# Moving the last quarter of w1's conversion behind the first products of a packed-attention mixer

## The chip, the cores and the metric

The kernel runs on one core of a Trainium2 chip. The metric is the device time of one launch in microseconds (us). Its engines are named as the profile names them: PE (TensorE, matrix products) with PEld (its weight loads), DVE (VectorE), ACT (ScalarE), POOL (GpSimd) and SP, the engine whose queue issues all of this kernel's transfers (SPq in the profile). Each engine works through its own instructions in order.

## The reference

An attention through 32 packed queries per head, then a token mix of low rank and a two-layer channel mix. Shapes: 8 batches, 8 heads, 576 tokens, head size 64, model width 512, hidden width 2048. U, V, w1 and w2 come as float64; the others as float32.

```python
def sm_attn(qq, kk, vv):                       # scale = 1/8
    s = scale * qq @ kk.T
    a = exp(s - max(s)); a = a / (sum(a) + 1e-9)
    return a @ vv
pp  = sm_attn(p, k, v)                         # 32 packed rows per head
x   = sm_attn(q, pp, pp)                       # (B, S, 512) after the heads are joined
h   = x.transpose(0, 2, 1) @ U @ V             # mixes tokens, rank 32
u   = x + h.transpose(0, 2, 1)
out = u + relu(u @ w1) @ w2
```

## The kernel before, in words

**First stage** (about the first 107 us). Sixteen *units* `u = (b, g)`, a batch and half of its heads each. For each unit the kernel loads a tile of k (`kx`, three buffers, `a_load`) and one of v (`vt`, three buffers, `a_load_v`), turns k on PE (`a_turn`, tiles `k_ps`), multiplies with the turned queries `pT` (`a_scores`, `s_ps`), takes maximum and exponential (`a_softmax`: DVE `mx`, ACT `e`), turns back, multiplies with v (`a_pack`: ACT `two`) and turns the packed rows (`a_heads`: ACT copies them into `ppTa`, one buffer, and SP stores `ppTa` to DRAM as `ppTd`). The raw packed queries `pn` are loaded for two batches at a time. Batch 0's own attention (`attention(0, res)`) runs among the units.

**Weights.** w1 and w2 are float64 in DRAM and are turned into float32 on the chip by `float32_of` (lines 71 to 82): one ACT instruction (absolute value, line 77 or 143) and four of DVE (lines 78 to 81) on a raw tile `bits` of 128x512 numbers, 512 KB. w1 has 16 such chunks, four for each quarter of the 2048 hidden columns. Before, all 16 are converted in the first stage, one after each unit's softmax and two at units 1, 5 and 9; each conversion (`some_w1`) is followed by the absolute value of the next chunk and the load of the third after it. Four chunks are loaded up front. The result stays in SBUF as `w1t`.

**Main stage.** For each batch `b` a loop over 16 steps `kt` of 128 hidden columns. `fold(b, c)` multiplies a quarter c of w1 with the batch's packed rows (line 372) and splits the result into a high and a low part, `wth` by ACT (line 378) and `wtl` by DVE (line 379); it runs at kt 2, 6, 10 and 14 for the quarter that is needed from the second step after on. So w1's last quarter is first read at kt = 10 of batch 0. `gemm1(kt)` makes the hidden columns in two PSUM banks `h_ps` (one buffer each, lines 86 to 88), ACT makes `hh` and `hj` of them (lines 611, 613) and DVE `hl` (line 614). `gemm1(kt + 1)` overwrites the same banks and so waits for `hl` of step kt. `gemm2(kt - 1)` (tiles `o`) follows `gemm1(kt)`.

**Batch 0 has more to do**: w2's 16 chunks are converted in it, one per step. At step kt `split_w2` writes the two parts of chunk kt + 1 (`w2h` by ACT, line 158; `w2l` by DVE, line 159), then chunk kt + 3 is loaded and chunk kt + 2 converted. The steps of `attention(1, res)` are handed out among these too (`steps`), and the tail of the last units (`rest`).

The order of the main stage is the order of the code (a manual schedule); the first stage's order is made by the framework's scheduler. Below, "step 3" means kt = 3 of batch 0, and gemm1(3) or hl(3) what belongs to it.

Of the kernel before, what the change touches and what calls it, by code (L numbers as in the profile page):

```python
# [8 lines left out]
F32 = mybir.dt.float32  # L9
F32R = mybir.dt.float32r  # L10
I32 = mybir.dt.int32
# [8 lines left out]
def packed_attention_mixer_kernel(  # L20
# [27 lines left out]
    nc = tc.nc  # L48
    B, H, S, D = q.shape
# [4 lines left out]
    P = 128  # L54
# [3 lines left out]
    NK = DF // P  # L58
    NU = 2 * B
    QW = 512  # L60
    NPC = DF // QW
# [7 lines left out]
    U, V, w1, w2 = (a.bitcast(I32) for a in (U, V, w1, w2))  # L69
# [35 lines left out]
    def ppT_tile():  # L105
        return pipe.tile([P, 2, P], F32, name="ppT", bufs=3)
# [6 lines left out]
    w1t = [pipe.tile([P, DF], F32, name=f"w1t{x}", tag=f"w1t{x}") for x in range(4)]  # L113
    w2t = {}

    def w2_tiles(pool, n):
        for i in range(n, n + 2):
            w2t[i] = tuple(pool.tile([P, 4, DM], F32R, name=f"w2{x}{i}", tag=f"w2{x}{i}", bufs=1) for x in "hl")
# [6 lines left out]
    def conv_tile(dtype):  # L125
        return pipe.tile([P, DM], dtype, name="os", bufs=4)
# [2 lines left out]
        return pipe.tile([P, 512, 2], I32, name="bits", bufs=2)  # L129

    chunks = [(x, c) for c in range(NPC) for x in range(4)]
    bits = {}

    def load_w1(n):
        x, c = chunks[n]
        b = bits["w1", n] = bits_tile() if n % 2 else sA.tile([P, 512, 2], I32, name="bits2")
        nc.sync.dma_start(out=b.rearrange("p x t -> p (x t)"), in_=w1[P * x:P * x + P, 2 * QW * c:2 * QW * c + 2 * QW])
# [15 lines left out]
    def convert_w2(kt):  # L153
        return kt, float32_of(conv_tile(I32), conv_tile(F32), bits.pop(("w2", kt)))
# [212 lines left out]
    def fold(b, c):  # L367
        f_ps = [bank() for _ in range(2)]
        for h in range(H):
            g, z = h // 4, h % 2  # L370
            xs, zs = slice(32 * (h % 4 ^ g), 32 * (h % 4 ^ g) + 32), slice(64 * z, 64 * z + 64)
            nc.tensor.matmul(f_ps[g][xs], lhsT=ppT[b][zs, g, xs], rhs=w1t[h // 2][zs, QW * c:QW * c + QW],  # L372
                             start=True, stop=True)
        for a in range(2):
            hi, lo = (pipe.tile([P, 2, QW // 2], F32R, name=f"wt{x}", tag=f"wt{x}", bufs=3) for x in "hl")
            cs = slice(QW // 2 * a, QW // 2 * a + QW // 2)
            for g in range(2):
                nc.scalar.copy(hi[:, g], f_ps[g][:, cs])  # L378
                nc.vector.tensor_tensor(lo[:, g], f_ps[g][:, cs], hi[:, g].bitcast(F32), op=ALU.subtract)  # L379
            wt[b, 2 * c + a] = hi, lo  # L380
# [6 lines left out]
    sT = tctx.enter_context(tc.tile_pool(name="sT", bufs=2, side="right", reuse_waits="tile"))  # L387
# [5 lines left out]
    pn, pT, pps, sums = {}, {}, {}, {}  # L393
# [4 lines left out]
    def a_load(u):  # L398
        b, g = UN[u]
        ua[u] = {}  # L400
        if u % 4 == 0:
            pn[b // 2] = sA.tile([P, 2, 2, D], F32, name="pn", bufs=1)
            nc.sync.dma_start(out=pn[b // 2], in_=p[b:b + 2].rearrange("b (g h) n d -> (h n) b g d", g=2))
        ua[u]["x"] = sA.tile([P, 2 * S], F32, name="kx", bufs=3)
        load_nat(ua[u]["x"], k, b, g)

# [10 lines left out]
    def a_p(b):  # L417
        t_ps = bank()
        pT[b] = sA.tile([P, 2, P], F32, name="pT")
        pd = sA.tile([P, 2, 2, D], F32, name="pd", bufs=1)  # L420
        nc.gpsimd.tensor_copy(pd, pn[b // 2][:, b % 2].unsqueeze(2).to_broadcast([P, 2, 2, D]))
        for i in range(2):
            nc.tensor.transpose(t_ps[:, P * i:P * i + P], pd[:, i].rearrange("p z d -> p (z d)"), ident)
        nc.scalar.activation(pT[b][:, 0], t_ps[:, :P], AF.Copy, scale=scale)
        dst, src = (a.rearrange("p (y z n) -> p z y n", y=2, z=2) for a in (pT[b][:, 1], t_ps[:, P:2 * P]))
        for z in range(2):
            nc.scalar.activation(dst[:, z], src[:, 1 - z], AF.Copy, scale=scale)
# [55 lines left out]
    def a_heads(u):  # L483
        b, g = UN[u]
        if g == 0:
            pps[b] = ppT_tile() if b == 0 else sT.tile([P, 2, P], F32, name="ppTa", bufs=1)
        z_ps = bank()
        nc.tensor.transpose(z_ps[:, :P], ua[u]["two"].rearrange("p z d -> p (z d)"), ident)
        nc.scalar.copy(pps[b][:, g], z_ps[:, :P])
        if g == 1:  # L490
            if b == 0:
                ppT[0] = pps[0]
            else:
                nc.sync.dma_start(out=ppTd[b], in_=pps[b].rearrange("p g n -> p (g n)"))
# [1 line left out]
    a_load(0)  # L496
    a_load(1)
    a_load_v(0)
    for n in range(4):
        load_w1(n)  # L500
    a_turn(0)
    first = attention(0, res)
    test_w1(0)

    def some_w1(n):
        convert_w1(n)
        if n + 1 < 16:
            test_w1(n + 1)
        if n + 4 < 16:
            load_w1(n + 4)  # L510

    n_w1 = 0
    for i in range(NU):
        if i > 0:
            a_turn_back(i - 1, bank_a("m"))
        a_scores(i)
        if i + 1 < NU:
            a_load_v(i + 1)
            a_turn(i + 1)
        if i + 2 < NU:  # L520
            a_load(i + 2)
        a_softmax(i)
        for _ in range(2 if i in (1, 5, 9) else 1):
            if n_w1 < 16:
                some_w1(n_w1)
                n_w1 += 1
        if i > 1:
            a_pack(i - 2, bank_a("m"))
        if i > 2:
            a_heads(i - 3)  # L530
        if i >= 4:
            for _ in range(3):
                if first:
                    first.pop(0)()
        if i == 2:
            uv = load_uv()
        if i == 3:
            prepare_uv(*uv)
        if i == 13:
            fold(0, 0)  # L540
        if i == 14:
            load_w2(0)
            load_w2(1)
            steps = attention(1, res)
            steps.pop(0)()
            split_w2(*convert_w2(0))
            load_w2(2)
# [111 lines left out]
    def joint(b, parts):  # L659

        oj = psO.tile([P, DM], F32, name="o", tag="o")
        for kt in range(NK):
            if kt % 4 == 0:
                hi, lo = parts.pop(0)
                if kt // 4 + 2 < NK // 4:
                    parts.append(joint_parts(b, kt // 4 + 2))
            cs = slice(P * (kt % 4), P * (kt % 4) + P)
            mm3(oj, (hi[:, cs], lo[:, cs]), w2_parts(kt), kt == 0, kt == NK - 1)
            if kt == 0:
                for i in range(2):  # L670
                    residual(oj, ajh[i], ajl[i], rdh[i], rdl[i])
        return oj

    def store_joint(b, oj):
        os_ = conv_tile(F32)
        nc.scalar.copy(os_, oj)
        for i in range(2):
            nc.sync.dma_start(out=out[b - 1 + i].rearrange("(i c) m -> c i m", c=NT)[8], in_=os_[I * i:I * i + I])

    w2x = convert_w2(1)  # L680

    for n in (20, 19, 18, 15, 15, 14, 13, 12, 12, 11, 5, 0, 0, 0, 0):
# [2 lines left out]
    for b in range(B):  # L685
        cur = Batch(b)
        oj = None
        ahead = attention(b + 2, res) if b + 2 < B else []
        for kt in range(NK):
            cur.gemm1(kt)  # L690
            if oj and kt == 1:
                store_joint(b - 1, oj)
            if steps and (b < 2 or kt % 4 != 2) and (b, kt) != (1, 0):
                steps.pop(0)()
            if (b, kt) == (0, 5):
                w2_tiles(ctx.enter_context(tc.tile_pool(name="sC", bufs=1, side="right", reuse_waits="tile")), 2)
            if kt > 0:
                cur.gemm2(kt - 1, (rest or steps).pop(0) if b == 0 and (rest or steps) else None)
            elif last:
                last.gemm2(NK - 1)  # L700
                last.store()
                if last.b % 2 == 1:
                    oj = joint(last.b, parts)
            if w2x:
                split_w2(*w2x)
                w2x = None
                if kt + 3 < NK:
                    load_w2(kt + 3)
                if kt + 2 < NK:
                    w2x = convert_w2(kt + 2)  # L710
            if kt % 4 == 2 and (b, kt) != (B - 1, NK - 2):
                n = b * NPC + kt // 4 + 1
                fold(n // NPC, n % NPC)
            elif steps and (b, kt) != (1, 0):
                steps.pop(0)()
            if kt == 1:
                cur.blocks()
            if kt == 3:
                cur.add_u()
            if ahead and kt == (13 if b else NK - 1):  # L720
                ahead.pop(0)()
            if kt == NK - 1 and b % 2 == 1:
                parts = [joint_parts(b, 0), joint_parts(b, 1)]
        assert not steps
        steps = ahead
        last = cur
# [35 lines left out]
```

## Time and profile before

| | before |
|---|---|
| time, median of 3 runs | 851.7 us (851.23 to 853.27) |
| time of the profiled execution | 849.79 us |
| its span, first to last instruction | 848.0 us |
| mean granted TensorE clock | 0.985 of full speed |
| busy in the span: PE / DVE / ACT / POOL | 815.2 / 381.2 / 327.8 / 86.1 us |
| start of gemm1(0), the main stage's first product | 107.39 us |

The page gives each engine's busy time and share, and the busy tenths in 40 slices of 21.2 us: PE stands at 9 in nearly all slices behind the fifth, DVE is high in the first nine and falls to 3 or 4 after them. The DMA engines are busy throughout the first four slices (tenths 9 9 9 9) and mostly idle later. The chain of work that ended last runs over PE for 85% of the span.

### The profile page before, as it was taken

To read this page: it belongs to the slowest core of one execution; us is meant where nothing else is said; L and a number is where in the kernel's file an instruction comes from. 1 tells how busy PE (TensorE), PEld (TensorE's weight loads), DVE (VectorE), ACT (ScalarE), POOL (GpSimd) and SP (SyncE) were. 2 spreads that over 40 slices of the span, in tenths; PEclk is the share of its full clock that TensorE was granted. 3 is DMA by queue.
4 is the path that set the end of the run, shared out by engine and by line. 5 is a ranking of instruction groups with operands and counts; after the bars stand their busy time and mean duration, and the time that the engine had idled before them with its cause. 6 is when DMAs were issued, how large, how long until landed. Compare 5 with 4: busy or idle time off the path is not lost.

```text
span 848.0 us, 14578 instructions
## 1 busy us (share of the span) xinstructions
PE 815.2 (96%) x5800; PEld 654.5 (77%) x5800; DVE 381.2 (45%) x902; ACT 327.8 (39%) x1017; POOL 86.1 (10%) x131
## 2 busy tenths in 40 slices
PE   5888789999999999999999999999999999999997
PEld 3555468788878878888888887888788888888786
DVE  5799576984343333434343234333434234342221
ACT  5677664445223333334333342333234322342231
POOL 1122210111111000110011001010101011000000
PEclk8799999999999999999999999999999999999999
DMA  9999632331001100011001100010001100010001
GB/s 306 353 346 313 229 104 71 104 131 50 1 1 63 51 13 1 1 63 50 1 2 63 50 14 1 17 61 36 1 3 61 63 1 1 2 50 1 1 1 63
DMA packets 36182, 58.13 MB, mean 69 GB/s; under 512 B 8977, under 2 KB 19217, under 8 KB 36113
## 3 DMA queue, kind: packets, MB, share of 16 engines
q1 hardware_dynamic: 36112, 57.19, 20.4%
q8 instruction: 46, 0.75, 0.4%
q14 instruction: 24, 0.19, 0.1%
HBM read 46.83 MB, written 10.35 MB: 67 GB/s over the span
## 4 chain that ended last, share of the span: by engine, by line
PE 85%; DVE 6%; DMA 4%; ACT 2%; issue 1%; SPq 1%; POOL 0%; ACTq 0%; POOLq 0%; DVEq 0%
PE o L86 16%; PE o L88 16%; PE o L87 16%; PE h_ps L86 8%; PE h_ps L88 7%; PE h_ps L87 7%; PE t_ps L372 4%; DMA vt<-in_v_dram 2%; DMA bits<-in_moe_w_ch_dram 2%; PE t_ps L224 2%; PE t_ps L244 1%; PE t_ps L320 1%; DVE os L80 1%; PE k_ps L224 1%; PE s_ps L244 1%
## 5 line engine op out<-in xcount | busy, mean ns | idle before, releaser
L86 PE MATMUL o<-w2h,hh 128*128 128x512 f32 x512 | 206.8, 404 | 0.0
L88 PE MATMUL o<-w2h,hl 128*128 128x512 f32 x512 | 202.5, 396 | 0.0
L87 PE MATMUL o<-w2l,hh 128*128 128x512 f32 x512 | 202.1, 395 | 0.0
L614 DVE SCALAR_TENSOR_TENSOR hl<-h_ps,hh 128x256 fp32r<-128x256 f32 x256 | 104.1, 423 | 203.3 <-ACT hj L613 191.2
L611 ACT ACTIVATE hh<-h_ps 128x256 fp32r<-128x256 f32 x256 | 99.0, 388 | 185.5 <-PE h_ps L88 184.9
L86 PE MATMUL h_ps<-ah,wth 128*128 128x320 f32 (+1 forms) x512 | 157.3, 307 | 1.7 <-DVE hl L614 1.7
L87 PE MATMUL h_ps<-al,wth 128*128 128x320 f32 (+1 forms) x512 | 151.7, 296 | 0.0
L88 PE MATMUL h_ps<-ah,wtl 128*128 128x320 f32 (+1 forms) x512 | 151.5, 296 | 0.0
L86 PEld LDWEIGHTS h_ps<-ah,wth 128*128 128x128 f32 x512 | 96.8, 189 | 33.3 <-issue 25.2
L88 PEld LDWEIGHTS o<-w2h,hl 128*128 128x128 f32 x512 | 96.5, 188 | 22.8
L86 PEld LDWEIGHTS o<-w2h,hh 128*128 128x128 f32 x512 | 96.8, 189 | 21.5 <-issue 4.6
L87 PEld LDWEIGHTS o<-w2l,hh 128*128 128x128 f32 x512 | 96.8, 189 | 16.7
L87 PEld LDWEIGHTS h_ps<-al,wth 128*128 128x128 f32 x512 | 96.9, 189 | 1.9
L88 PEld LDWEIGHTS h_ps<-ah,wtl 128*128 128x128 f32 x512 | 97.0, 190 | 0.0
L379 DVE TENSOR_TENSOR wtl<-t_ps,wth 128x256 fp32r<-128x256 f32 x128 | 48.5, 420 | 92.8 <-ACT wth L378 89.5
L378 ACT CAST wth<-t_ps 128x256 fp32r<-128x256 f32 x128 | 43.4, 374 | 111.1 <-PE t_ps L372 97.8
L335 POOL TENSOR_TENSOR al<-aT,ah 128x320 fp32r<-128x320 f32 (+1 forms) x32 | 25.9, 812 | 206.4 <-ACT ah L334 206.4
L283 POOL TENSOR_TENSOR e<-e,m 128x576 f32<-128x576 f32 x16 | 18.9, 1184 | 257.1 <-DVE m L282 257.1
L372 PE MATMUL t_ps<-w1t,ppT 64*32 64x512 f32 x512 | 36.8, 608 | 0.0
L231 ACT COPY xT<-t_ps 128x256 f32<-128x256 f32 x60 | 20.3, 394 | 39.6 <-PE t_ps L224 39.0
L334 ACT CAST ah<-aT 128x320 fp32r<-128x320 f32 (+1 forms) x32 | 13.8, 433 | 44.5 <-DVE aT L333 44.5
L294 POOL TENSOR_TENSOR e<-e,s 128x576 f32<-128x576 f32 x16 | 18.9, 1179 | 109.8 <-DVE s L293 102.7
(134 smaller groups left out, 964.2 us busy)
## 6 DMA issues: line engine op xcount, KB each, us to landing
bits<-in_moe_w_ch_dram SPq DMA_DIRECT2D x32, 512.0 KB, 6.3
kx<-in_k_dram SPq DMA_DIRECT2D x16, 576.0 KB, 7.2
x<-in_q_dram SPq DMA_DIRECT2D x16, 576.0 KB, 4.9
vt<-in_v_dram SPq DMA_DIRECT2D x32, 256.0 KB, 6.7
out_dram<-bits SPq DMA_DIRECT2D x32, 256.0 KB, 2.4
vt<-in_v_dram SPq DMA_DIRECT2D x16, 64.0 KB, 6.0
out_dram<-os SPq DMA_DIRECT2D x8, 128.0 KB, 2.3
ppTd<-ppTa SPq DMA_DIRECT2D x7, 128.0 KB, 4.0
```

Source lines behind the costliest of these rows:

```text
L86: nc.tensor.matmul(ps, lhsT=lh, rhs=rh, start=start, stop=False)
L87: nc.tensor.matmul(ps, lhsT=lh, rhs=rl, start=False, stop=False)
L88: nc.tensor.matmul(ps, lhsT=ll, rhs=rh, start=False, stop=stop)
L224: nc.tensor.transpose(t_ps[:, o:o + P], x[:, h, P * j:P * j + P], ident)
L231: nc.scalar.copy(dst, src[:, a])
L283: nc.gpsimd.tensor_tensor(e, e, m.unsqueeze(2).to_broadcast([P, S // 32, 32]), op=ALU.subtract)
L335: nc.gpsimd.tensor_tensor(al[:, g, ns], aT[:, ns], ah[:, g, ns].bitcast(F32), op=ALU.subtract)
L372: nc.tensor.matmul(f_ps[g][xs], lhsT=ppT[b][zs, g, xs], rhs=w1t[h // 2][zs, QW * c:QW * c + QW], start=True, stop=True)
L378: nc.scalar.copy(hi[:, g], f_ps[g][:, cs])
L379: nc.vector.tensor_tensor(lo[:, g], f_ps[g][:, cs], hi[:, g].bitcast(F32), op=ALU.subtract)
L611: nc.scalar.activation(hh[:, ms], src, AF.Relu)
L614: nc.vector.scalar_tensor_tensor(hl[:, ms], src, 0.0, hh[:, ms].bitcast(F32), op0=ALU.max, op1=ALU.subtract)
```

## The change

- The `pn` load brings one batch's packed queries instead of two, at every first unit of a batch.
- `ppTa` has two buffers instead of one.
- Two chunks of w1 are loaded up front instead of four. Units 0 and 1 convert nothing and load chunks 2 and 3; units 2 to 13 convert one chunk each: 12 chunks, three quarters of w1.
- The last quarter is converted in 8 halves of 128x256 numbers in batch 0, two in each of steps 3 to 6, called h0 to h7 below: one behind the first attention step of kt, one behind w2's conversion. A half's raw tile `wb` (256 KB) has one buffer. h0 is loaded at step 2; each conversion issues the load of the next half.
- In steps 2, 6, 10 and 14 the fold stands ahead of `split_w2` and w2's conversion, where it stood behind them.

```diff
+    NA = 4 * (NPC - 1)
+    halves = [(x, c, hf) for x, c in chunks[NA:] for hf in range(2)]
...
-        if u % 4 == 0:
-            pn[b // 2] = sA.tile([P, 2, 2, D], F32, name="pn", bufs=1)
...
+        if g == 0:
+            pn[b] = sA.tile([P, 2, D], F32, name="pn", bufs=1)
+            nc.sync.dma_start(out=pn[b], in_=p[b].rearrange("(g h) n d -> (h n) g d", g=2))
...
-            pps[b] = ppT_tile() if b == 0 else sT.tile([P, 2, P], F32, name="ppTa", bufs=1)
+            pps[b] = ppT_tile() if b == 0 else sT.tile([P, 2, P], F32, name="ppTa")
...
-    for n in range(4):
-        load_w1(n)
+    load_w1(0)
+    load_w1(1)
...
+    turns = [0, 0] + [1] * NA + [0, 0]
...
-        for _ in range(2 if i in (1, 5, 9) else 1):
-            if n_w1 < 16:
-                some_w1(n_w1)
-                n_w1 += 1
+        if i < 2:
+            load_w1(2 + i)
+        for _ in range(turns[i]):
+            some_w1(n_w1)
+            n_w1 += 1
...
+    def load_half():
+        x, c, hf = halves[0]
+        b = bits["half"] = sB.tile([P, QW // 2, 2], I32, name="wb", bufs=1)
+        c0 = 2 * QW * c + QW * hf
+        nc.sync.dma_start(out=b.rearrange("p x t -> p (x t)"), in_=w1[P * x:P * x + P, c0:c0 + QW])
+
+    def convert_half():
+        x, c, hf = halves.pop(0)
+        c0 = QW * c + QW // 2 * hf
+        float32_of(conv_tile(I32)[:, :QW // 2], conv_tile(F32)[:, :QW // 2], bits.pop("half"),
+                   w1t[x][:, c0:c0 + QW // 2])
+        if halves:
+            load_half()
...
+            if b == 0 and 3 <= kt < 7:
+                convert_half()
             if kt > 0:
                 cur.gemm2(kt - 1, (rest or steps).pop(0) if b == 0 and (rest or steps) else None)
...
+            if kt % 4 == 2 and (b, kt) != (B - 1, NK - 2):
+                n = b * NPC + kt // 4 + 1
+                fold(n // NPC, n % NPC)
             if w2x:
                 split_w2(*w2x)
...
                 if kt + 2 < NK:
                     w2x = convert_w2(kt + 2)
-            if kt % 4 == 2 and (b, kt) != (B - 1, NK - 2):
-                n = b * NPC + kt // 4 + 1
-                fold(n // NPC, n % NPC)
-            elif steps and (b, kt) != (1, 0):
+                if b == 0 and kt == 2:
+                    load_half()
+                if b == 0 and 3 <= kt < 7:
+                    convert_half()
+            if steps and kt % 4 != 2 and (b, kt) != (1, 0):
                 steps.pop(0)()
```

Line numbers of the changed kernel are up to 22 higher in the main loop (its hl is line 620, its hh line 617, its w2h line 161, its w2l line 162). The order of the instructions on three engines shows where the work goes.

**SP, the opening of the kernel**, before (bits is a chunk of w1, kx of k, vt of v):

```order
L403 DMA pn<-in_p_dram 128x4x64
L211 DMA kx<-in_k_dram 128x2x576 x2
L413 DMA vt<-in_v_dram 64x4x256 x2
L415 DMA vt<-in_v_dram 64x4x64
L137 DMA bits_110<-in_moe_w_ch_dram 128x1024
L137 DMA bits<-in_moe_w_ch_dram 128x1024
L137 DMA bits_114<-in_moe_w_ch_dram 128x1024
L137 DMA bits<-in_moe_w_ch_dram 128x1024
L413 DMA vt<-in_v_dram 64x4x256 x2
L415 DMA vt<-in_v_dram 64x4x64
L211 DMA kx<-in_k_dram 128x2x576
```

and after:

```order
L406 DMA pn<-in_p_dram 128x2x64
L214 DMA kx<-in_k_dram 128x2x576 x2
L416 DMA vt<-in_v_dram 64x4x256 x2
L418 DMA vt<-in_v_dram 64x4x64
L140 DMA bits_110<-in_moe_w_ch_dram 128x1024
L140 DMA bits<-in_moe_w_ch_dram 128x1024
L416 DMA vt<-in_v_dram 64x4x256 x2
L418 DMA vt<-in_v_dram 64x4x64
L406 DMA pn<-in_p_dram 128x2x64
L214 DMA kx<-in_k_dram 128x2x576
L140 DMA bits_185<-in_moe_w_ch_dram 128x1024
```

Two chunks of w1 that stood ahead of the second v tile and the third k tile now stand behind them.

**DVE in step 3** (batch 0), before, from hl(3) to hl(4):

```order
L614 SCALAR_TENSOR_TENSOR hl<-h_ps_1980,hh 128x256
L614 SCALAR_TENSOR_TENSOR hl<-h_ps_1990,hh 128x256
L159 TENSOR_TENSOR w2l_87<-os,w2h_86 128x512
L78 TENSOR_SCALAR os<-os 128x512
L79 TENSOR_SCALAR os<-os 128x512
L80 SCALAR_TENSOR_TENSOR os<-bits,os 128x512
L81 SCALAR_TENSOR_TENSOR os<-bits,os 128x512
L614 SCALAR_TENSOR_TENSOR hl<-h_ps_2087,hh 128x256
```

and after, from behind hl(3) on (h0, then w2's parts and conversion, then the start of h1, behind which hl(4) comes):

```order
L78 TENSOR_SCALAR os<-os 128x256
L79 TENSOR_SCALAR os<-os 128x256
L80 SCALAR_TENSOR_TENSOR os<-wb,os 128x256
L81 SCALAR_TENSOR_TENSOR w1t_80<-wb,os 128x256
L162 TENSOR_TENSOR w2l_87<-os,w2h_86 128x512
L78 TENSOR_SCALAR os<-os 128x512
L79 TENSOR_SCALAR os<-os 128x512
L80 SCALAR_TENSOR_TENSOR os<-bits,os 128x512
L81 SCALAR_TENSOR_TENSOR os<-bits,os 128x512
L78 TENSOR_SCALAR os<-os 128x256
L79 TENSOR_SCALAR os<-os 128x256
```

Eight instructions of DVE are new between hl(3) and hl(4), and each group of four needs the raw half `wb` to be there.

**ACT from step 3's w2 conversion on**, before (os<-bits is the absolute value of a chunk of w2):

```order
L77 ACTIVATE os<-bits 128x512
L235 COPY xT<-t_ps 64x4x64
L611 ACTIVATE hh<-h_ps_2087 128x256
L613 ACTIVATE hj<-h_ps_2087 128x64
L611 ACTIVATE hh<-h_ps_2097 128x256
L489 COPY ppTa<-t_ps 128x128
L158 CAST w2h_86<-os 128x512
L77 ACTIVATE os<-bits 128x512
L611 ACTIVATE hh<-h_ps_2152 128x256
```

and after:

```order
L77 ACTIVATE os<-bits 128x512
L77 ACTIVATE os<-wb 128x256
L238 COPY xT<-t_ps 64x4x64
L617 ACTIVATE hh<-h_ps_2079 128x256
L619 ACTIVATE hj<-h_ps_2079 128x64
L617 ACTIVATE hh<-h_ps_2089 128x256
L77 ACTIVATE os<-wb 128x256
L492 COPY ppTa<-t_ps 128x128
L161 CAST w2h_86<-os 128x512
L77 ACTIVATE os<-bits 128x512
L77 ACTIVATE os<-wb 128x256
L617 ACTIVATE hh<-h_ps_2162 128x256
```

The absolute values of the halves h1, h2 and h3 now stand in ACT's queue ahead of `hh` of step 4, of w2h, and of `hh` of step 5.

## Rows read from the trace of the kernel before

**Rows 1.** Busy time by stretch: window, length, then busy us (xcount) of each engine.

```profile
core 0: us, PE busy (x) PEld busy (x) DVE busy (x) ACT busy (x) POOL busy (x), PEclk, DMA share, GB/s
5.00:80.00 75.00, 61.68 (x855) 39.85 (x856) 61.31 (x140) 49.00 (x147) 14.55 (x27) 0.86 1.05 347
...
143.90:176.00 32.10, 31.37 (x203) 24.39 (x201) 30.27 (x61) 16.09 (x43) 4.60 (x5) 1.00 0.29 95
...
190.00:848.00 658.00, 651.71 (x4047) 536.85 (x4046) 236.41 (x587) 215.92 (x691) 53.35 (x64) 1.00 0.07 25
```

**Rows 2.** The page's DMA issues: count, size of one, median us to landing.

```profile
bits<-in_moe_w_ch_dram SPq DMA_DIRECT2D x32, 512.0 KB, 6.3
out_dram<-bits SPq DMA_DIRECT2D x32, 256.0 KB, 2.4
```

**Rows 3.** DVE in time order, first stage's tail: start, us, instruction, [idle before].

```profile
93.52 0.81 DVE L78 TENSOR_SCALAR os<-os 128x512 f32<-128x512 f32 x1 [0.59 <-ACT os L77]
```

**Rows 4.** PE in time order, places where it waits or a step begins.

```profile
98.25 0.87 PE L250 MATMUL m_ps<-ident,e 128*128 128x128 f32 x4 [2.73 <-ACT e L450]
...
110.95 0.41 PE L86 MATMUL h_ps<-ah,wth 128*128 128x320 f32 x1 [1.70 <-DVE hl L614]
...
126.17 0.63 PE L224 MATMUL t_ps<-ident,x 128*128 128x128 f32 x4 [1.31 <-DVE wtl L379]
...
176.00 0.42 PE L86 MATMUL h_ps<-ah,wth 128*128 128x320 f32 x1
```

**Rows 5.** The chain of waits around gemm1(0): start, us, what.

```profile
107.02 2.67 DMA ppTd<-ppTa
...
109.77 0.27 ACT ppTa L489
```

**Rows 6.** DVE in time order, steps 2 to 11 of batch 0.

```profile
124.74 1.61 DVE L379 TENSOR_TENSOR wtl<-t_ps,wth 128x256 fp32r<-128x256 f32 x4
126.33 0.76 DVE L614 SCALAR_TENSOR_TENSOR hl<-h_ps,hh 128x256 fp32r<-128x256 f32 x2
130.22 0.69 DVE L159 TENSOR_TENSOR w2l<-os,w2h 128x512 fp32r<-128x512 f32 x1 [3.13 <-ACT w2h L158]
...
135.27 0.97 DVE L614 SCALAR_TENSOR_TENSOR hl<-h_ps,hh 128x256 fp32r<-128x256 f32 x2 [2.10 <-ACT hj L613]
...
138.61 0.69 DVE L159 TENSOR_TENSOR w2l<-os,w2h 128x512 fp32r<-128x512 f32 x1 [1.62 <-ACT w2h L158]
...
141.48 0.74 DVE L282 TENSOR_REDUCE m<-e 128x18 f32<-128x576 f32 x1
...
143.87 0.69 DVE L159 TENSOR_TENSOR w2l<-os,w2h 128x512 fp32r<-128x512 f32 x1 [0.99 <-ACT w2h L158]
...
153.91 0.76 DVE L614 SCALAR_TENSOR_TENSOR hl<-h_ps,hh 128x256 fp32r<-128x256 f32 x2
...
175.52 0.76 DVE L614 SCALAR_TENSOR_TENSOR hl<-h_ps,hh 128x256 fp32r<-128x256 f32 x2
```

**Rows 7.** ACT in time order, the first two wth of step 2's fold.

```profile
123.11 0.65 ACT L378 CAST wth<-t_ps 128x256 fp32r<-128x256 f32 x2 [0.68 <-PE t_ps L372]
```

**Rows 8.** Conversion on DVE and ACT by form: xcount | busy us, mean ns | idle before.

```profile
L78 DVE TENSOR_SCALAR os<-os 128x160 f32<-128x160 f32 x1 | 0.2, 236 | 0.0
L79 DVE TENSOR_SCALAR os<-os 128x512 int32<-128x512 int32 x32 | 14.0, 438 | 0.7
L80 DVE SCALAR_TENSOR_TENSOR os<-x,os 128x160 int32<-128x160 int32 x1 | 0.3, 314 | 0.0
L80 DVE SCALAR_TENSOR_TENSOR os<-bits,os 128x512 int32<-128x512 int32 x32 | 22.3, 698 | 0.7
...
L77 ACT ACTIVATE os<-bits 128x512 f32<-128x512 f32 x16 | 10.9, 681 | 0.0
L77 ACT ACTIVATE os<-x 128x160 f32<-128x160 f32 x1 | 0.4, 378 | 0.0
```

**Rows 9.** Loads of w2 from 95 to 195 us (line 151), issue to landing.

```profile
DMA to landing us min/median/max: 3.4/3.5/4.1
```

More of the change, by code (lines that the diff above doesn't have):

```diff
@@ L400, in a_load @@
         ua[u] = {}
-        if u % 4 == 0:
-            pn[b // 2] = sA.tile([P, 2, 2, D], F32, name="pn", bufs=1)
-            nc.sync.dma_start(out=pn[b // 2], in_=p[b:b + 2].rearrange("b (g h) n d -> (h n) b g d", g=2))
+        if g == 0:
+            pn[b] = sA.tile([P, 2, D], F32, name="pn", bufs=1)
+            nc.sync.dma_start(out=pn[b], in_=p[b].rearrange("(g h) n d -> (h n) g d", g=2))
         ua[u]["x"] = sA.tile([P, 2 * S], F32, name="kx", bufs=3)
@@ L420, in a_p @@
         pd = sA.tile([P, 2, 2, D], F32, name="pd", bufs=1)
-        nc.gpsimd.tensor_copy(pd, pn[b // 2][:, b % 2].unsqueeze(2).to_broadcast([P, 2, 2, D]))
+        nc.gpsimd.tensor_copy(pd, pn[b].unsqueeze(2).to_broadcast([P, 2, 2, D]))
         for i in range(2):
@@ L506, in some_w1 @@
         convert_w1(n)
-        if n + 1 < 16:
+        if n + 1 < NA:
             test_w1(n + 1)
-        if n + 4 < 16:
+        if n + 4 < NA:
             load_w1(n + 4)
+    turns = [0, 0] + [1] * NA + [0, 0]
     n_w1 = 0
```

## The prediction

> **What bounds the kernel now.** I read the busy times by stretch first, then PE's and DVE's instructions in time order, then the chain of waits and the transfers. From 5 to 80 us the DMA engines are busy all the time at 347 GB/s, and DVE is busy for 61.31 of 75 us [rows 1]: the first stage is bound by its loads and, among its units, by DVE. From 190 us on PE is busy for 651.71 of 658 us [rows 1] and nothing in the change touches that. Between lies batch 0, where w2 is converted. The reader should look at DVE there: from 143.9 to 176 us it is busy for 30.27 of 32.1 us [rows 1], and hl(11) starts at 175.52, its first half (0.42 us) ends at 175.94, and PE's gemm1(12), which needs that bank, starts at 176.00 [rows 4, 6]. So DVE and PE are level there: the slack is 0.06 us, and what is added to DVE's queue ahead of that point delays PE almost one for one, unless it falls into DVE's gaps. Between hl(3) and hl(7) there are four gaps: 3.13, 2.10, 1.62 and 0.99 us, together 7.84 [rows 6].
>
> The sum is made against the profiled execution (849.79 us, span 848.0). The median is 851.7, 1.9 higher; I add that at the end.
>
> **First stage: what goes out.** Four chunks of w1 of 512 KB each [rows 2] are 2.10 MB. At 347 GB/s [rows 1] that is 6.0 us. Two of these four stood at the front of the queue, ahead of the third k tile; there the gain is certain, 2 x 0.52 MB / 347 = 3.0 us. In the middle DVE paces too, and the order shows about as many conversions there as before (ten between the maxima of units 3 and 10, nine before), so the other 3.0 us come only if the loads pace. In the tail, a conversion of w2 starting at 93.52 stands in front of a unit's maximum, and PE waits 2.73 us, until 98.25, for the exponential behind it [rows 3, 4]; in the new order it stands in front of an earlier unit's maximum, and no conversion lies between the last units. I take half of that wait, 1.4 us, since the next latency of the tail is close. Sum: 6.0 + 1.4 = 7.4 us earlier. Bounds: 3.0 (only the opening) and 9.2 (four conversions of DVE at 2 x 0.44 + 2 x 0.70 = 2.3 us each [rows 8], should DVE alone have been the pace). Four absolute values less on ACT lie beside this. The smaller pn loads (four more issues on SP, the same bytes) I cost at nothing: SP runs ahead of a busy DMA; without that cover, four issues, under 2 us, inside the bounds.
>
> **The second ppTa.** PE waits 1.70 us at 110.95 for hl(0) [rows 4]. The chain shows why: ACT's ppTa copy waited for the store of the one before (2.67 us from 107.02), and hh(0) stands behind it on ACT [rows 5]. With a second buffer the copy doesn't wait. hh, hj and hl still take their time after gemm1(0), so I take 1.5 (bounds 0 and 1.7) off.
>
> **Batch 0: the fold first.** In step 2 PE waits 1.31 us for wtl, which DVE begins at 124.74 behind w2's conversion [rows 4, 6]. With the fold in front it begins with the first wth, which ACT starts at 123.11 [rows 7] and ends 0.36 later: at 123.5, 1.25 us earlier, and PE gets that back. But DVE then has nothing to do while it waits for wth, and w2l and the conversion follow wtl: 2.87 us, as from 138.61 to 141.48 [rows 6]. wtl ends at 125.1, w2l waits for w2h until 125.3, hl(3) follows at 128.15 and ends at 128.9, where it ended at 127.09 before (126.33 + 0.76 [rows 6]). (All on the clock of before, with the earlier start left out.)
>
> **Batch 0: the halves.** One half on DVE: the trace has this code at 160 and 512 columns, 0.236 and 0.438 us for lines 78 and 79, 0.314 and 0.698 for 80 and 81 [rows 8]; on a straight line 256 columns take 0.29 and 0.42. Four in a row with three gaps of 0.03: 1.51 us, or 1.43 of pitch. Eight are 11.4 us, against 7.84 us of gaps. The absolute value on ACT, between 0.378 and 0.681 [rows 8]: 0.46.
>
> The price is not in these but in the load. `wb` has one buffer: the next half's load is issued when DVE has read this one, ACT's absolute value waits for it to land, DVE's four for ACT, and all queues are in order. So from one half's start to the next: 1.51 conversion + 0.05 to issue + landing + 0.46 + 0.05. A load of w2, 512 KB, lands 3.5 us after issue in this stretch [rows 9]; half the bytes save 0.26 MB / 347 = 0.75, so I take 2.7. Bounds: 2.4, the median of 256 KB stores [rows 2], and 3.5. The cycle is 1.51 + 0.05 + 2.7 + 0.46 + 0.05 = 4.77 us. What stands between two halves on DVE is shorter than the waiting part of 3.26: w2l and conversion 2.87, or hl and an attention step about 1.6. So h0 starts at 128.9 and h6 at 128.9 + 6 x 4.77 = 157.5. Between h6 and h7 stands more (wtl 1.61, w2l and conversion 2.87, and attention's sum with its reciprocal: a reduction of 0.74 like the one at 141.48 and two small instructions, say 1.2 [rows 6]), so h7 doesn't wait: h6 1.43 + 1.2 + 1.61 + 2.87 + h7 1.43 = 8.5, and hl(7) starts at 166.0. Before it started at 153.91 [rows 6]: 12.1 us later. Who waits: on ACT, hh(5) stands behind the absolute value of h3, w2h behind h2; on DVE, hl(5) behind h3; on PE, gemm1(6) waits for hl(5), gemm1(7) for hl(6), gemm1(8) for hl(7). From hl(7) to hl(11) DVE has no gap over 0.8 us in which to make it good, so gemm1(12) starts 12.1 - 0.06 = 12.0 us later. Behind that PE paces again and keeps the loss. Bounds by the landing: 6 x 0.3 less, 10.2, and 6 x 0.8 more, 16.8.
>
> A load of 512 KB lands 3.5 us after its issue [rows 9], and with one buffer a half's landing lies whole between two halves. The Trainium skill, "Trainium Kernel Development and Optimization", Best Practices, tells the kernel's author to double-buffer so that transfers run beside compute; it speaks against this `wb`, and no run here shows how two would do. "DMA: Bandwidth & Descriptors", Anatomy of one DMA, gives about 2.0 us fixed plus bytes over 436 GB/s for one issued by GpSimd: an estimate of 3.2 us for 512 KB, where the trace has 3.5, and of 2.6 for 256 KB, by which hl(7) would come 0.6 us sooner.
>
> **Sum.** -7.4 - 1.5 + 12.0 = +3.1: 852.9 for the profiled execution, and with 1.9 for the median **854.8 us**. Later folds cost and give nothing: DVE has room and the w2 conversion is over.
>
> **The rivals.**
> 1. *The loads hide, the first stage's gain stays: not slower.* If SP issued a half early enough for it to land under DVE's other work, only the 11.4 us of conversion count. DVE's work between hl(3) and hl(7) was 26.82 us (127.09 to 153.91) less the 7.84 of gaps: 18.98. 128.9 + 18.98 + 11.4 = 159.3, 5.4 us late. Sum -7.4 - 1.5 + 5.3 = -3.6: 848.1. It decides from a landing of about 1.1 us (4.77 - 2.7 + 1.1 = 3.2, a step's DVE work per half). Against it: no load or store in the page's median lands under 2.4 us [rows 2]. For it: PE's and DVE's gaps may be laid better than I see, and the first stage may give its 9.2.
> 2. *The first stage doesn't shorten with its loads.* DVE and the order of the units pace it from the third unit on, and only the opening's 3.0 us come: -3.0 - 1.5 + 12.0 = +7.5: 859.2. For it: DVE's share in the middle and the conversions that were moved there. Against it: the DMA engines are busy throughout.
>
> **How the numbers follow.** The forecast case 0.57, with an own range of 850.5 to 860; rival 1, 0.20; rival 2, 0.15; 0.08 for both signs of what I don't see. A measurement of this kernel can tell 0.3%, 2.55 us, from no change: the limits are 849.15 and 854.25. Slower: 0.32 of the forecast case (its centre lies just above the limit), 0.15, 0.04: 0.51. Same: 0.22 of the forecast case and 0.07 of rival 1: 0.29. Faster: 0.03, 0.13, 0.04: 0.20. The range reaches from rival 1 with a better first stage, 845.5, to the landing's upper bound and rival 2, 862.
>
> **What would show it.** Right: gemm1(0) at about 100 us; no wait before gemm1(1); DVE idle ahead of the halves' first instruction with ACT's absolute value as releaser, and ACT idle on the `wb` load, some 3 us each time; halves 4.8 us apart; PE waits of 2 to 4 us for hl before gemm1(6), (7) and (8); gemm1(12) at 176.0 + 12.0 - 7.4 - 1.5 = 179.1. Wrong: halves that follow closely without idle time (rival 1), a gemm1(0) at 104 (rival 2), or a `wb` load that lands far from 2.7 us.

## The result and the profile after

The changed kernel takes **854.74 us** (854.12 to 859.0, six executions) against 851.64 (850.45 to 853.27): a ratio of 1.0043, 95% interval 1.0023 to 1.0063. It is 3.1 us slower; the forecast was 854.8.

The profiled execution of the changed kernel is its slowest (859.0 us, span 857.2): from 50 to 70 us the granted clock is 0.50 to 0.75, behind a wait of PE of 1.87 us at 49.68, and about 3 us go there. The wait alone doesn't explain it: it is 1.86 or 1.87 us in experiments 1, 2, 7 and 9 too, and there the clock is back at 1.00 from 54 to 68 us. Why it stayed low for longer here isn't shown. The other executions have spans of 852.3 to 853.7. So its batch 0 is read below, while the first stage is read from five experiments whose instructions stand in the same order up to batch 0.

```profile
core 0: us, PE busy (x) PEld busy (x) DVE busy (x) ACT busy (x) POOL busy (x), PEclk, DMA share, GB/s
50.00:55.00 5.00, 5.00 (x58) 3.71 (x59) 4.90 (x8) 2.30 (x5) 2.07 (x2) 0.66 1.06 356
55.00:60.00 5.00, 3.35 (x42) 1.63 (x32) 4.85 (x13) 3.67 (x14) 1.84 (x3) 0.75 0.60 213
60.00:65.00 5.00, 5.00 (x37) 2.98 (x37) 3.79 (x7) 1.39 (x4) 0.30 (x1) 0.50 0.79 238
65.00:70.00 5.00, 5.00 (x59) 2.96 (x58) 2.99 (x7) 3.42 (x9) 0.72 (x3) 0.50 0.69 207
```

These are windows of the changed kernel (columns as in rows 1). The reader should see PE full at half the clock in the last two windows, while the transfers run at 238 and 207 GB/s; in the same windows of experiment 2, at a clock of 1.00 and 0.94, they ran at 288 and 273, and from 5 to 80 us at 347 before [rows 1].

PE in time order, changed kernel: gemm1(0), (1) and (6), the scores of batch 1's attention behind step 6's fold, gemm1(8) and (12):

```profile
103.31 0.42 PE L86 MATMUL h_ps<-ah,wth 128*128 128x320 f32 x1
...
105.50 0.42 PE L86 MATMUL h_ps<-ah,wth 128*128 128x320 f32 x1 [0.33 <-DVE hl L620]
...
141.74 0.41 PE L86 MATMUL h_ps<-ah,wth 128*128 128x320 f32 x1 [3.38 <-DVE hl L620]
...
158.38 1.09 PE L247 MATMUL t_ps<-xT,ppT 64*32 64x320 f32 x16 [2.69 <-DVE wtl L382]
...
163.47 0.63 PE L86 MATMUL h_ps<-ah,wth 128*128 128x320 f32 x1 [1.57 <-DVE hl L620]
...
185.20 0.41 PE L86 MATMUL h_ps<-ah,wth 128*128 128x320 f32 x1 [0.76 <-DVE hl L620]
```

The waits of 2.73 us in the tail and of 1.70 us before gemm1(1) [rows 4] are gone, the second down to 0.33. In their place stand waits of 3.38, 2.69 and 1.57 us in steps 6 to 8, all released by DVE. gemm1(12) comes 9.2 us later than before, and so does the end of the span (857.2 against 848.0): behind it nothing is made good.

DVE in time order, changed kernel: wtl of step 2, hl(3), the first instruction of h0, h1, h2, h3, h6 and h7, then hl(7):

```profile
118.05 1.62 DVE L382 TENSOR_TENSOR wtl<-t_ps,wth 128x256 fp32r<-128x256 f32 x4 [1.92 <-ACT wth L381]
...
122.63 0.75 DVE L620 SCALAR_TENSOR_TENSOR hl<-h_ps,hh 128x256 fp32r<-128x256 f32 x2
123.30 0.28 DVE L78 TENSOR_SCALAR os<-os 128x256 f32<-128x256 f32 x1
...
128.67 0.29 DVE L78 TENSOR_SCALAR os<-os 128x256 f32<-128x256 f32 x1 [0.99 <-ACT os L77]
...
133.54 0.29 DVE L78 TENSOR_SCALAR os<-os 128x256 f32<-128x256 f32 x1 [1.91 <-ACT os L77]
...
139.15 0.29 DVE L78 TENSOR_SCALAR os<-os 128x256 f32<-128x256 f32 x1 [1.21 <-ACT os L77]
...
154.37 0.30 DVE L78 TENSOR_SCALAR os<-os 128x256 f32<-128x256 f32 x1 [2.69 <-ACT os L77]
...
161.54 0.29 DVE L78 TENSOR_SCALAR os<-os 128x256 f32<-128x256 f32 x1
163.00 0.75 DVE L620 SCALAR_TENSOR_TENSOR hl<-h_ps,hh 128x256 fp32r<-128x256 f32 x2
```

Each half up to h6 finds DVE idle until ACT's absolute value; h7 does not. From h0 to h6 it is 31.07 us, 5.18 a half. hl(3) to hl(7) takes 40.37 us, where it took 27.58 [rows 6]: 12.8 more. The view of the tile `wb` names the cause, ACT's wait for the load, and its landing:

```profile
  DMA wb<-in_moe_w_ch_dram: 21.4, 7
...
  ACT os L77: 21.4, 7
  DVE os L78: 9.8, 6
...
DMA to landing us min/median/max: 2.7/3.2/3.7
```

### The profile page after: what moved, and what is told of

Read it like the earlier page. It is cut to its first block, busy times and chain, and to the rows that moved or that the text cites. A ratio compares the mean times of both kernels' runs of the same rounds, so it can differ in the third digit from the quotient of the medians.

```text
span 857.2 us, 14619 instructions
## 1 busy us (share of the span) xinstructions
PE 822.8 (96%) x5800; PEld 658.8 (77%) x5800; DVE 385.3 (45%) x918; ACT 327.6 (38%) x1021; POOL 88.2 (10%) x131
## 4 chain that ended last, share of the span: by engine, by line
PE 87%; DMA 6%; DVE 4%; ACT 2%; issue 1%; SPq 0%; ACTq 0%
PE o L86 16%; PE o L88 16%; PE o L87 16%; PE h_ps L86 9%; PE h_ps L88 8%; PE h_ps L87 8%; PE t_ps L375 4%; DMA wb<-in_moe_w_ch_dram 2%; DMA bits<-in_moe_w_ch_dram 2%; PE t_ps L247 2%; PE t_ps L227 1%; PE t_ps L323 1%; PE m_ps L481 1%; DMA vt<-in_v_dram 1%; DMA x<-in_moe_U_dram 1%
```

## The experiments

**The theory** was that the halves cost their load's landing, since one buffer lets the next load start only when DVE has read the last. **The rival** was that DVE's added work, or ACT's queue, costs. The ratios below are to the kernel before, run on the same chip. The experiments ran on three chips, on which the kernel before took 850.97 to 851.93 us, so a difference between two experiments can be off by up to 1 us.

**1. A second raw buffer.** It lies in slots of `hj` that are free until step 8.

```diff
-        b = bits["half"] = sB.tile([P, QW // 2, 2], I32, name="wb", bufs=1)
+        if i == 0:
+            b = sB.tile([P, QW // 2, 2], I32, name="wb", bufs=1)
+        else:
+            b = hj[:, 4 + 4 * i:8 + 4 * i].rearrange("p k x -> p (k x)").rearrange("p (x t) -> p x t", t=2).bitcast(I32)
...
-                    load_half()
+                    for _ in range(2):
+                        load_half()
```

> The changed kernel with a second buffer for the raw halves (laid into four slots of hj that batch 0 fills only from its step 8 on): two halves are loaded at step 2, and each conversion issues the load of the half after the next. Nothing else moves on PE, and DVE and ACT keep their order. Landing theory: a load then has two cycles less one conversion to land, 2 x 3.3 - 1.5 = 5.1 us against 3.2, so ACT's waits for wb (21.4 us) go, the halves follow at what DVE has to do, and batch 0 costs about 5.4 us instead of 12: 854.7 - 6.6 = 848 us (846.5 to 850). Rival (DVE's added 11.4 us of conversion are what costs, or ACT's queue is): within 1 us of the changed kernel, 854 to 855.5.

Measured: 846.47 us (845.34 to 848.84), ratio 0.9947 (0.9929 to 0.9965), 8.3 us less than the changed kernel. In the tile's view ACT's waits are 1.3 us for `wb` (and 1.1 for the buffer in `hj`), with loads that land no sooner:

```profile
  DMA wb<-in_moe_w_ch_dram: 1.3, 2
...
DMA to landing us min/median/max: 3.0/3.4/3.6
```

The landing theory holds and the rival falls as the main cause.

**2. No quarter, and 3. the halves alone.** Experiment 2 is the changed kernel without the halves. It leaves the last quarter out: the fold multiplies the third quarter in its place, with the same work for the engines and another result.

```diff
-            nc.tensor.matmul(f_ps[g][xs], lhsT=ppT[b][zs, g, xs], rhs=w1t[h // 2][zs, QW * c:QW * c + QW],
+            nc.tensor.matmul(f_ps[g][xs], lhsT=ppT[b][zs, g, xs], rhs=w1t[h // 2][zs, QW * min(c, 2):QW * min(c, 2) + QW],
...
-            if b == 0 and 3 <= kt < 7:
-                convert_half()
...
-                if b == 0 and kt == 2:
-                    load_half()
-                if b == 0 and 3 <= kt < 7:
-                    convert_half()
```

> The changed kernel without the eight halves: no load and no conversion of w1's last quarter at all; the fold of the last quarter reads the third quarter in its place, which leaves its work on the engines as it is. What is left is the first stage's gain, the second ppTa and the fold's place. Landing theory: 12.0 us less than the changed kernel, about 842.7 (841 to 845), so 9 us under the kernel before. Rival (only DVE's work counts, 5.4 us): about 849.3, 2.4 under the kernel before. If the first stage gains only its opening's 3.0 us, the kernel before less 4.5, 847.

Measured: 841.42 us (840.56 to 843.96), ratio 0.9889 (0.9872 to 0.9906). The halves cost 854.74 - 841.42 = 13.3 us with one buffer, and 846.47 - 841.42 = 5.05 with two: 8.3 of the 13.3 are the single buffer, 5 are what the halves cost without it. With each time taken against the kernel before of its own runs the 13.3 is 12.9; between the two profiles, from gemm1(0) to gemm1(12), it is 81.89 - 67.24 = 14.65. So it is good to about 1 us.

Experiment 3 is the kernel before with `load_half`, `convert_half` and their three calls added as the change has them; the quarter is converted twice.

```diff
+            if b == 0 and 3 <= kt < 7:
+                convert_half()
...
+                if b == 0 and kt == 2:
+                    load_half()
+                if b == 0 and 3 <= kt < 7:
+                    convert_half()
```

> The kernel before, first stage and fold as they were, with the eight halves of w1's last quarter loaded and converted once more among steps 3 to 6 as in the changed kernel (one wb buffer). This is the batch 0 term alone. Landing theory: h0 starts behind hl(3) at 127.1, h6 6 x 4.77 later, the rest as in the prediction: 10.3 us more than the kernel before, 862 (860 to 865; by the measured spacing of 5.2 us instead of 4.77, 864.5). Rival (DVE's work only): 11.4 less 7.84 of gaps, 3.6 us more, 855.2.

Measured: 866.6 us (866.01 to 867.86), ratio 1.0181 (1.0164 to 1.0199): 15.4 more, above the expected 860 to 865. hl(3) to hl(7) is 41.32 us there, 13.7 longer than before. Of the remaining 1.7 us the trace places 1.1 behind hl(7): from there to gemm1(12) it is 23.23 us, 22.09 before. PE has waited 6.65 us for wtl, the clock is 0.57 from 170 to 175 us, and DVE idles 0.53 us for `hj` ahead of hl(8). The rest I can't assign.

**4. The fold in front, alone.**

```diff
+            if kt % 4 == 2 and (b, kt) != (B - 1, NK - 2):
+                n = b * NPC + kt // 4 + 1
+                fold(n // NPC, n % NPC)
             if w2x:
                 split_w2(*w2x)
...
-            if kt % 4 == 2 and (b, kt) != (B - 1, NK - 2):
-                n = b * NPC + kt // 4 + 1
-                fold(n // NPC, n % NPC)
-            elif steps and (b, kt) != (1, 0):
+            if steps and kt % 4 != 2 and (b, kt) != (1, 0):
```

> The kernel before with only the fold moved ahead of w2's parts and conversion in steps 2, 6, 10 and 14. By the prediction PE gets the second and third bank of step 2's fold 1.25 us earlier, and DVE ends hl(3) about 1.8 us later since it waits for wth; hl(4) and the later ones take that up in DVE's gap of 3.13 us. PE is level with DVE only later: within 1 us of the kernel before, 851 to 852.5. Rival: the 1.8 us reach hl(11) and the end, 853.4; or the 1.25 us are kept, 850.4.

Measured: 851.68 us (849.3 to 854.61) against 851.22, ratio 1.0008 (0.9996 to 1.0019). It is worth nothing that can be told from zero.

**5. The turned packs' buffer, alone.** In the kernel before, batch 6's packs go into an idle buffer, and the order of PE, DVE and SP is untouched.

```diff
-            pps[b] = ppT_tile() if b == 0 else sT.tile([P, 2, P], F32, name="ppTa", bufs=1)
+            pps[b] = ppT_tile() if b in (0, 6) else sT.tile([P, 2, P], F32, name="ppTa", bufs=1)
```

> The kernel before with one edit: the turned packs of batch 6 go into the third buffer of ppT, which is idle then, instead of the one ppTa, so that ACT's copy ahead of gemm1(0)'s hh doesn't wait for the store of batch 5. PE, DVE and SP keep their order; the copy now stands one place earlier on ACT. This is the second term of the prediction alone. If only the wait counts, 1.4 to 1.5 us: 851.9 - 1.5 = 850.4. If most executions of the kernel before also have the dip of the granted clock that followed the waits of 2.17 and 2.39 us (1.5 us more on PE by the matmuls of 0.63 instead of 0.40 us): 851.9 - 3 = 849.

Measured: 848.04 us (846.98 to 849.21) against 850.97, ratio 0.9961 (0.9946 to 0.9976): 2.9 us, not 1.5. Experiment 4 has the single buffer; its gemm1(1), two products of gemm2(0) and gemm1(2) on PE, and the windows behind the wait (columns as in rows 1, the clock behind POOL's), are these:

```profile
111.55 0.41 PE L86 MATMUL h_ps<-ah,wth 128*128 128x320 f32 x1 [2.17 <-DVE hl L614]
...
113.74 0.63 PE L86 MATMUL o<-w2h,hh 128*128 128x512 f32 x1
114.16 0.63 PE L87 MATMUL o<-w2l,hh 128*128 128x512 f32 x1
...
118.65 0.31 PE L86 MATMUL h_ps<-ah,wth 128*128 128x320 f32 x1
```

```profile
112.00:114.00 2.00, 2.00 (x12) 2.00 (x11) 1.93 (x4) 0.91 (x4) 0.00 (x0) 0.65 0.00 0
114.00:116.00 2.00, 2.00 (x6) 1.39 (x5) 1.42 (x4) 0.36 (x1) 0.00 (x0) 0.50 0.04 8
```

The same of experiment 5:

```profile
110.15 0.42 PE L86 MATMUL h_ps<-ah,wth 128*128 128x320 f32 x1 [0.33 <-DVE hl L614]
...
111.85 0.40 PE L86 MATMUL o<-w2h,hh 128*128 128x512 f32 x1
112.08 0.40 PE L87 MATMUL o<-w2l,hh 128*128 128x512 f32 x1
...
115.72 0.31 PE L86 MATMUL h_ps<-ah,wth 128*128 128x320 f32 x1
```

```profile
112.00:114.00 2.00, 2.00 (x44) 1.37 (x45) 1.93 (x5) 0.39 (x1) 0.00 (x0) 1.00 0.03 8
114.00:116.00 2.00, 2.00 (x17) 1.65 (x18) 0.95 (x3) 1.64 (x5) 0.47 (x2) 1.00 0.12 41
```

Behind a wait of 2.17 us the clock falls to 0.50 (1.2 GHz) and a product starts every 0.42 instead of 0.23 us. From gemm1(1) to gemm1(2) it is 7.10 us instead of 5.57: the dip costs 1.5 us on top of the wait. The profiled execution of before, with 1.70 us [rows 4], had no dip; all three profiles of its variants with this buffer (experiments 4, 6 and 3, waits of 2.17, 2.17 and 2.39 us) had one.

The same edit undone in the changed kernel (`ppTa` with one buffer again) is not as clean, since the scheduler then orders the tail differently.

```diff
-            pps[b] = ppT_tile() if b == 0 else sT.tile([P, 2, P], F32, name="ppTa")
+            pps[b] = ppT_tile() if b == 0 else sT.tile([P, 2, P], F32, name="ppTa", bufs=1)
```

> The changed kernel with one ppTa buffer again, as in the kernel before; everything else as changed (the scheduler puts some instructions of the units' tail in another order). If the second buffer is worth the 1.5 us of the prediction: 854.7 + 1.5 = 856.2 us. If the wait for the store also costs what follows it in the two runs in which it was 2.17 and 2.39 us long (the granted clock at 0.50 to 0.72 for the next 4 us, some 1.5 us more on PE): 857.5 to 858.5, with that dip behind gemm1(1) in the trace.

Measured: 857.49 us (ratio 1.0068, 1.0048 to 1.0087), 2.75 more than the changed kernel. But its profile shows a wait of 1.22 us before gemm1(1) and no dip, and gemm1(0) at 100.97; so not all of the 2.75 is this wait, and the run decides nothing.

**6. The opening's loads.** All 16 chunks stay in the first stage; one doubled conversion moves along, from unit 1 to unit 2.

```diff
-    for n in range(4):
-        load_w1(n)
+    load_w1(0)
+    load_w1(1)
...
-        for _ in range(2 if i in (1, 5, 9) else 1):
+        if i < 2:
+            load_w1(2 + i)
+        for _ in range(2 if i in (2, 5, 9) else 1):
```

> The kernel before with only the opening's loads moved: two chunks of w1 up front and chunks 2 and 3 behind the loads of units 2 and 3; all 16 chunks are still loaded and converted in the first stage, two at units 2, 5 and 9 (the scheduler puts no conversion between the last four maxima). No half, no second ppTa, fold as before. By the prediction's terms: the opening's 3.0 us and no fewer bytes, and of the tail's 2.73 us wait about 1.4: 851.2 - 4.4 = 846.8. If the opening's gain is given back because the same bytes have to come later (the loads pace throughout): 851.2 - 1.4 = 849.8, or no change. If the whole tail gain of the changed kernel (3.7 us from the maximum of unit 12 to gemm1(0)) comes with it: 844.5.

Measured: 850.99 us against 851.93, ratio 0.9985 (0.9975 to 0.9996). DVE's maxima of units 2, 5, 6 and 12 in this kernel:

```profile
21.55 0.76 DVE L448 TENSOR_REDUCE mx<-s_ps 128x1 f32<-128x576 f32 x1 [0.32 <-PE m_ps L478]
...
40.48 0.76 DVE L448 TENSOR_REDUCE mx<-s_ps 128x1 f32<-128x576 f32 x1
51.93 0.75 DVE L448 TENSOR_REDUCE mx<-s_ps 128x1 f32<-128x576 f32 x1
...
92.12 0.75 DVE L448 TENSOR_REDUCE mx<-s_ps 128x1 f32<-128x576 f32 x1
```

Before, these started at 24.36, 45.46, 51.18 and 90.45. A lead of 2.8 to 5 us is lost within one unit, the one behind 40.48, where the transfers run at 345 GB/s (columns as in rows 1):

```profile
40.00:52.00 12.00, 8.52 (x101) 5.77 (x109) 8.92 (x21) 7.45 (x24) 1.41 (x5) 0.86 1.07 345
```

DVE is busy for 8.92 of the 12 us and the DMA engines all the time, which fits that the same bytes come later; that the conversions don't share in it isn't shown.

**7. Two buffers, and the halves earlier.** The buffers are those of experiment 1; the cut shows what is new.

```diff
-            if b == 0 and 3 <= kt < 7:
+            if b == 0 and 2 <= kt < 6:
                 convert_half()
...
-                if b == 0 and kt == 2:
+                if b == 0 and kt == 0:
...
-                if b == 0 and 3 <= kt < 7:
+                if b == 0 and kt in (1, 3, 4, 5):
```

> The version with two raw buffers, with the halves moved forward: the first two loads at step 0, one half converted behind w2's conversion in step 1, one behind hl(2) (in DVE's wait of 1.92 us for wth in step 2), then two in each of steps 3 to 5. In the version with two buffers DVE has no gap from 116.9 to 166 us, so that its work there sets the pace, and it has gaps before 116.9 (1.05, 1.92 us). Theory (DVE's work is what is left of the cost): 2 x 1.43 us leave the full stretch and lie in the gaps, so 846.5 - 2.5 = 844 us (843 to 845). Rival (what is left of the 5 us is contention or ACT, not DVE's queue): 846.5, and hl(2) later by 1.4 us gives a new wait of PE before gemm1(3): 847.5.

Measured: **843.32 us** (842.64 to 843.55), ratio 0.9894 (0.9878 to 0.9911), 1.1% faster than the kernel before and 11.4 us faster than the changed one; 1.9 us above the kernel without any half, which ran on another chip (2.7 us between the two profiles, 1.2 with each against its own kernel before). A wait of PE of 0.98 us in step 2 is new. So most of what two buffers leave of the cost is DVE's queue in the crowded steps.

**8. Two buffers, eight of w2's low parts on POOL.** The buffers are again those of experiment 1.

```diff
-        (nc.gpsimd if kt == 0 else nc.vector).tensor_tensor(lo, x, hi.bitcast(F32), op=ALU.subtract)
+        (nc.gpsimd if kt == 0 or 4 <= kt < 12 else nc.vector).tensor_tensor(lo, x, hi.bitcast(F32), op=ALU.subtract)
```

> The version with two raw buffers, with w2's low part (w2l) of chunks 4 to 11 on POOL instead of DVE, 1.27 us there against 0.69 us on DVE each. If DVE's work is all that counts: 6 of the 8 lie in the full stretch, 6 x 0.69 = 4.1 us less, 842.5. Rival: DVE's line 78 took 0.82 and 1.38 us instead of 0.28 and 0.42 in the trace of that version where POOL subtracted the maximum at the same time; if each w2l on POOL holds up line 78 or 79 so, 0.5 to 1.0 us are given back each time, and the time stays at 846 to 848.

Measured: 849.38 us (848.44 to 851.38), ratio 0.9972 (0.9962 to 0.9981): 2.9 us worse than experiment 1 (2.2 with each against its own kernel before). POOL and DVE at one place of it:

```profile
121.23 1.30 POOL L162 TENSOR_TENSOR w2l<-os,w2h 128x512 fp32r<-128x512 f32 x1 [0.46 <-ACT w2h L161]
...
121.25 1.43 DVE L79 TENSOR_SCALAR os<-os 128x256 int32<-128x256 int32 x1
122.71 0.43 DVE L80 SCALAR_TENSOR_TENSOR os<-wb,os 128x256 int32<-128x256 int32 x1
...
126.09 0.29 DVE L79 TENSOR_SCALAR os<-os 128x256 int32<-128x256 int32 x1
```

The DVE instruction that meets POOL's takes 1.43 instead of 0.29 us. That is 1.14 lost for 0.69 saved, and it happens to lines 78, 80 and 81 too (1.06 instead of 0.42, 1.67 instead of 0.69, and 1.52 instead of 0.42). Each of the eight subtractions meets one such instruction and costs it 0.6 to 1.1 us, about 7.0 in all, for 5.5 saved; the rest of the loss is in part a new idle time of DVE, 2.1 us, for ACT's absolute values. The Trainium skill, "SBUF — State Buffer", section "SBUF: two separate sides", says that the two engines share a pair of ports as an exclusive lock, held for a whole instruction, against DVE instructions with two inputs from SBUF as well; this trace agrees, with line 81's 1.52 us.

**9. One buffer, one half per step.**

```diff
-            if b == 0 and 3 <= kt < 7:
+            if b == 0 and 2 <= kt < 10:
                 convert_half()
...
-                if b == 0 and kt == 2:
+                if b == 0 and kt == 0:
                     load_half()
-                if b == 0 and 3 <= kt < 7:
-                    convert_half()
```

> The changed kernel with its one raw buffer, but one half per step, in steps 2 to 9 behind hl, instead of two in each of steps 3 to 6; the first load at step 0. A load then has a whole step (about 5 us) less the conversion's 1.5 to land, where it needs 3.2. If it is the time between issue and use that costs, and not the one buffer as such, the loads hide as with two buffers, and the one half at step 2 falls into DVE's wait for wth: 854.7 - 8 = 846.5 (845 to 848). If each half costs its landing wherever it stands (ACT's queue blocked): 854 to 856.

Measured: 846.2 us (845.59 to 846.76), ratio 0.9939 (0.9927 to 0.9952). In the tile's view ACT still waits 7.7 us, three times, for a landing as long as before, and DVE only 0.6:

```profile
  DMA wb<-in_moe_w_ch_dram: 7.7, 3
...
  DVE os L78: 0.6, 2
...
DMA to landing us min/median/max: 2.9/3.2/3.5
```

So one buffer is enough where a load has the time between two uses to land. The spreading does a second thing, which this run doesn't part from the first: it takes halves out of the crowded steps, one of them into step 2's gap. What the halves in steps 7 to 9 add is paid there: hl(7) to gemm1(12) takes 26.74 us instead of 22.21.

## Why the prediction was right

The mechanisms held where they were tested, with one split wrong inside the first stage. Two terms were mis-sized by about as much in opposite directions, so that the total was met to 0.1 us is partly luck. Term by term, with the prices from the experiments:

| term | predicted | measured | from |
|---|---|---|---|
| first stage to gemm1(0) | -7.4 | -7.62 | traces, below |
| second ppTa | -1.5 | -2.93 | experiment 5 |
| fold in front | in the next | +0.46 (not told from 0) | experiment 4 |
| halves | +12.0 | +13.32 | experiment 2 |
| sum | +3.1 | +3.23 (3.10 as medians) | |

**First stage: the sum was right, its split wrong.** gemm1(0) starts between 99.51 and 100.95 us (mean 100.06) in the five experiments with the changed first stage, and between 107.39 and 107.96 (mean 107.68) in four profiles with the old one. Experiment 2's:

```profile
99.51 0.41 PE L86 MATMUL h_ps<-ah,wth 128*128 128x320 f32 x1
```

The prediction called the opening's 3.0 us certain; experiment 6, 0.9 us in all, shows that they are not kept when the bytes stay. In the kernel of experiment 2 the lead is 3.0 us at unit 2 (21.32 against 24.36), 4.2 at unit 12 (86.27 against 90.45), and 7.9 at gemm1(0). So the middle gave 1.1 where 3.0 were counted, and the tail 3.7 where 1.4 were. The tail's 3.7 is more than the whole wait of 2.73 us that went: in all four profiles of the old stage the clock behind that wait is 0.50 or 0.51 from 100 to 102 us, and in experiments 1 and 2, which don't wait there, it is 1.00 from 84 to 100. The prediction priced the wait and not the clock behind it. Rival 2 (only the opening) is out. Whether loads or DVE pace the middle was not settled; taking four chunks out removes both. The one unit shown in experiment 6 speaks for the loads.

**Second ppTa: mis-sized by 1.4.** The mechanism was right. The term rested on one execution, which waited 1.70 us; the executions that wait over 2 us pay the dip of the clock as well. From gemm1(0) to gemm1(12) it is 67.23 us in experiment 5, 68.61 in the profile of before and 70.59 and 70.62 in experiments 4 and 6, which have the dip: 1.4 us for the wait alone and 3.4 with the dip, and the measured 2.9 lies between. It would also fit that the profiled execution of before, which has no dip, lies 1.9 us under the median. Then the 1.9 us that the prediction added at the end for the median stood for a dip that the second ppTa takes away, and the halves' longer landing made up for it.

**Fold.** DVE's idle time before wtl in step 2 is 1.92 us, as the order of the rows said, and later gaps take it up: hl(3) to hl(7) takes 25.70 us in experiment 4 instead of 27.58.

**Halves: the chain was right, the landing was mis-sized.** 2.7 us was taken, the 3.5 of twice the bytes [rows 9] less the time of half of them; it is 3.2 by the median. The cycle is 5.18 instead of 4.77 us, six of them 2.5 us longer, inside the bound of 0.8 a half. Against rival 1 the prediction said that no load or store of the page lands under 2.4 us by the median; the page has 128 KB stores at 2.3, which changes nothing here. That h7 wouldn't wait was right. The predicted gemm1(12) at 179.1 against 185.20 is made of these 2.5 and of the 3.3 us by which this execution's first stage was late; 0.3 us are left over. PE's waits for hl came before gemm1(6), 3.38 us, and before gemm1(8), 1.57, less than the 2 to 4 us that were said; before gemm1(7) PE waited for the attention's copies instead (1.49 us), and the 2.69 us for wtl behind step 6 were not foreseen.

**Rival 1** (only conversion counts, +5.4 us, total 848.1) is what experiment 1 makes of the kernel: +5.05. It said that it decides by whether a load can land under DVE's other work, and that is what experiments 1 and 9 changed.

## What to carry to other kernels

When a conversion is moved into another phase, count the load that feeds it: with one raw buffer that is refilled only after use, each piece takes its landing (3.2 us here) beside its 1.5 us of work, and what DVE's other work doesn't fill of it is lost (9.8 us of idle time over six halves here). Issue it a step earlier, by a second buffer or by spreading the pieces; either turned a loss of 3 us into a gain of 5, and using the gaps that DVE had before the crowded steps brought it to over 8. And price a stall from more than one execution: one that is 1.7 us long in the profile at hand can be 2.2 in most, and cost more than its length.

## What the runs showed of the hardware

- Waits of PE of 2.17, 2.17 and 2.39 us before gemm1(1) were each followed by a granted clock that fell to 0.50 (1.2 GHz); waits of 1.22 and 1.70 us at the same place were not. The length of the wait alone doesn't decide: a wait of 1.86 us at 48.9 us in experiment 2 was followed by 0.50 from 50 to 52 us, and one of 2.39 us before gemm1(8) in the run of experiment 5 that decides nothing, at 161.8 us, by 1.00 from 162 to 170.
- A POOL subtraction of 1.3 us holds up the DVE instruction beside it by 0.6 to 1.1 us (experiment 8), about as much or more than the 0.69 us of DVE's work that it takes over.
